# A decode step on one core: the last group's transposes ahead of the third group's normalization, its copies on two engines

## The chip, the core and the metric

The kernel runs on one core of a Trainium2 chip. A core has five engines that run side by side: TensorE (PE in the profile, with its weight loads as PEld), VectorE (DVE), ScalarE (ACT), GpSimd (POOL) and SyncE (SP), which here only issues transfers. Each has its own instruction queue, executed in order, and the queues meet at semaphores. Sixteen DMA engines bring data from the HBM memory to SBUF. TensorE writes its results to PSUM. The metric is the time of one execution in device microseconds; lower is better.

## What is computed

One token x of 576 values goes through a layer norm, and the result through two branches that are added to x. Cut to what matters:

```python
xn = _layernorm(x)
# A: attention over the last W = 4096 cached positions, 32 query heads on 16 key/value heads
q = (xn @ wq)                                  # 32 heads of 128
scores = einsum(q, k) * Dh ** -0.5
p = softmax(scores)
o = einsum(p, v)
a = o.reshape(B, Sq, Hq * Dh) @ wo
# B: gated unit, F = 4608
z = gelu(xn @ w_in); z1, z2 = z[..., :Fh], layernorm(z[..., Fh:])
b = (z1 * (w_sp * z2 + b_sp)) @ w_out
out = x + a + b
```

Everything is bf16 in memory. The keys and values of the window are 16 MB each, the weights some 17 MB more; each byte is used once.

## The kernel before

The 16 key/value heads are worked off in four groups (g = 0 to 3) of four heads. SyncE issues all large transfers in one order: wq, K of groups 0 and 1, w_in, then K and V in turn, and at the end the output weights: w_out (16 of its 18 tiles of 128 rows) and wo (32 tiles, in five transfers of 14, 9, 6, 2 and 1). Four large SBUF slots take turns, so a transfer waits until the last reader of its slot is done. The last two tiles of w_out come by two indirect transfers that GpSimd issues (`load_ext`, into `ext`).

The order of the work is written out by hand (`manual_schedule`): each engine's queue is the order of the Python calls. For each group the steps are:

- `keys` and `scores`: VectorE transposes K in blocks (L313), TensorE multiplies with the queries into S (L320).
- `sm_a`: VectorE takes the maximum over S and spreads it (L341 to L344), ScalarE writes the exponentials to `pz` and their sums to `lx` (L347).
- `sm_b`: VectorE transposes `pz` to `pt` in two instructions (L358), then ScalarE puts 32x128 pieces of `pt` in their places in `PT` with 16 copies, each from one block of 32 partitions to one block of 32 partitions (L361).
- `sums`, `recip`: TensorE adds `lx` over the partitions (L367), VectorE takes the reciprocal (L374, L375).
- `pv`: TensorE multiplies `PT` with V into the one PSUM tile `ops` (L384).
- `norm`: VectorE multiplies `ops` with the reciprocal and a mask (L394, into `om`) and adds up the columns (L398, into `on`). This frees `ops` for the next group.
- `y_mms`, `y_copy`: TensorE moves `on` to its place in a column (L405), VectorE writes it to Y (L412).

`recip`, `norm`, `y_mms` and `y_copy` together are `tail`. The small PSUM tiles (`lps`, `hx_ps`, `yps`) share one buffer (`ps_m`), so each waits until the one allocated before it has been read.

The other branch ends in `hv`, of which two columns are moved to other partitions for `ext` (`hx`). The output row is gathered in two PSUM tiles `acc` by matmuls with one column of `hv` or Y as weights (L530): `out_hv(0)`, `out_hv(1)` and `out_hv(2)` take the 16 tiles of w_out (12 + 12 + 8 matmuls), the last loop takes the 32 tiles of wo with Y, and the `ext` tiles after the 14th. Two casts (L549, L550) and one transfer bring the row out.

Of the kernel before, what the change touches and what calls it, by code (L numbers as in the profile page):

```python
# [23 lines left out]
GK = 4  # L24
NG = HKV // GK
# [20 lines left out]
def kernel(  # L46
# [14 lines left out]
    nc = tc.nc  # L61
# [243 lines left out]
    st = {}  # L305
# [45 lines left out]
    def sm_b(g):  # L351
        pt = single.tile([P, TC, 32], FP32, name=f"pt{g}", tag="pt")
        src = pz[:].rearrange("p t r x e -> p (t r x e)").bitcast(FP32)
        dst = pt[:].rearrange("p t x -> p (t x)")
        PT = work.tile([P, TC, GK, 2, 2], BF16, name=f"PT{g}", tag="PT")
        PT4 = PT[:].rearrange("p t x h e -> p (t x h e)").bitcast(FP32).rearrange("p (t x h) -> p t x h", x=GK, h=2)
        for n in range(2):
            nc.vector.transpose(dst[:, 1024 * n:1024 * (n + 1)], src[:, 1024 * n:1024 * (n + 1)])  # L358
        for x in range(GK):
            for a in range(4):  # L360
                nc.scalar.copy(PT4[32 * a:32 * a + 32, :, x, :], pt[32 * x:32 * x + 32, :, 2 * a:2 * a + 2])  # L361
        st[g]["PT"] = PT

    def sums(g):

        lps = ps_m.tile([P, 32], FP32, name=f"lps{g}", tag="m")
        nc.tensor.matmul(lps[:, 0:1], lhsT=lsum[:].rearrange("p v y e -> p (v y e)"), rhs=lx[:, g:g + 1],  # L367
                         start=True, stop=True)
        st[g]["lps"] = lps

    def recip(g):

        rs = work.tile([P, 1], FP32, name=f"rs{g}", tag="rs")
        nc.vector.tensor_scalar_max(rs[:], st[g]["lps"][:, 0:1], 0.5)  # L374
        nc.vector.reciprocal(rs[:], rs[:])  # L375
        st[g]["rs"] = rs

    def pv(g):

        d = st[g]  # L380
        for tb in range(8):
            for q in range(4):
                t0 = 32 * q + 4 * tb
                nc.tensor.matmul(  # L384
                    ops[32 * q:32 * q + 32, :],
                    lhsT=d["PT"][:, t0 // 2:t0 // 2 + 2].rearrange("p t x h e -> p (t x h e)"),
                    rhs=V[g][:, t0:t0 + 4, :],
                    start=(tb == 0), stop=(tb == 7), tile_position=(0, 32 * q),
                )

    def norm(g):
        d = st[g]
        om = work.tile([P, 4, DH], FP32, name=f"om{g}", tag="om")
        nc.vector.scalar_tensor_tensor(out=om[:].rearrange("p c d -> p (c d)"), in0=ops[:],  # L394
                                       scalar=d["rs"][:, 0:1], in1=dmask[:].rearrange("p c d -> p (c d)"),
                                       op0=ALU.mult, op1=ALU.mult)
        on = work.tile([P, DH], FP32, name=f"on{g}", tag="on")
        nc.vector.reduce_sum(on[:], om[:].rearrange("p c d -> p d c"), axis=AXX)  # L398
        d["on"] = on

    def y_mms(g):
        d = st[g]
        yps = ps_m.tile([P, 32], FP32, name=f"yps{g}", tag="m")
        for dq in range(4):
            nc.tensor.matmul(  # L405
                yps[32 * g:32 * g + 32, :], lhsT=sel[:, dq, :], rhs=d["on"][:, 32 * dq:32 * dq + 32],
                start=(dq == 0), stop=(dq == 3), tile_position=(0, 32 * g),
            )
        d["yps"] = yps

    def y_copy(g):
        nc.vector.tensor_copy(Y[32 * g:32 * g + 32, :], st[g]["yps"][32 * g:32 * g + 32, :])  # L412
# [59 lines left out]
    def tail(g):  # L472
        recip(g)
        norm(g)
        y_mms(g)
        y_copy(g)

    for g in range(2):
        for c in range(2):
# [4 lines left out]
            if g == 1 and c == 0:  # L484
                sm_a(0)
    zps = z_mms()
    sm_b(0)
    sm_a(1)
    keys(2, 0)
    scores(2, 0)  # L490
    sm_b(1)
    zg = z_exp(zps)
    keys(2, 1)
# [9 lines left out]
    pv(0)  # L503
    sm_a(2)
    tail(0)
    keys(3, 0)
    scores(3, 0)
    sm_b(2)
    sums(1)
    pv(1)  # L510
    keys(3, 1)
    scores(3, 1)
    tail(1)
    sm_a(3)
    hv = z_norm(G, sz)
    load_ext()
    sums(2)
    pv(2)
    tail(2)
    sm_b(3)  # L520
    hx_ps = ps_m.tile([P, 32], FP32, name="hx_ps", tag="m")
    nc.tensor.matmul(hx_ps[:, 0:NX], lhsT=move[:], rhs=hv[:, NM:NF], start=True, stop=True)
    hx = more.tile([P, NX], BF16, name="hx")
    nc.vector.tensor_copy(hx[:], hx_ps[:, 0:NX])  # L524
    sums(3)
    pv(3)

    def out_mms(lhs, col, wv, last):
        for n in range(2):
            nc.tensor.matmul(acc[n], lhsT=lhs[:, col:col + 1], rhs=wv[:, CUT[n]:CUT[n + 1]],  # L530
                             start=False, stop=last, tile_position=(0, 32 * n))

    def out_hv(c):
        for t, wv in wout_sb[6 * c:6 * c + 6]:
            out_mms(hv, t, wv, False)

    out_hv(0)
    out_hv(1)
    tail(3)
    out_hv(2)  # L540
    for t, wv in wo_sb:
        out_mms(Y, t, wv, t == 31)
# [39 lines left out]
```

## Time and profile before

| | us |
|---|---|
| time, median of 3 runs | 127.38 (126.96 to 127.93) |
| profiled execution, its own time | 126.47 |
| its span | 124.5 |
| VectorE busy | 80.9 (65%) |
| TensorE busy | 69.1 (55%) |
| ScalarE busy | 43.2 (35%) |
| GpSimd busy | 12.7 (10%) |
| HBM read | 51.25 MB, 412 GB/s over the span |

The span runs from the first to the last instruction of the program in one profiled execution; the execution's own time is longer by what lies around it. Times within the trace count from the span's start. In the page's list of groups a line gives the code line, engine and operation, what is written from what with partitions x elements, the count, the busy time and mean duration, and after the bar the idle time of the engine before these instructions with what ended it. In a timeline a line gives start, duration, engine, line, operation and count, and in brackets the idle time before it. The chain that ended last is followed backwards from the last instruction, at each step to what released it.

### The profile page before, as it was taken

The numbers are of one execution on the slowest core, as the hardware profiler recorded it, in microseconds if no ns is written. First come the engines' busy times: TensorE is split into PE (matmuls) and PEld (weight loads), VectorE is DVE, ScalarE is ACT, GpSimd is POOL, SyncE is SP. The second block draws the span as 40 slices with busy tenths as digits, with TensorE's granted clock in tenths as the row PEclk, the third lists the DMA queues.
The fourth block names the chain that finished last, engine by engine and source line by source line (L and its number), as shares of the span: only waits on it lengthen the run. The fifth ranks groups of instructions, "written<-read, shape, count | busy, mean of one in ns | idle before, by whom it ended". The sixth has DMA issues, their size and how long they took to land.

```text
span 124.5 us, 1494 instructions
## 1 busy us (share of the span) xinstructions
PE 69.1 (55%) x545; PEld 21.6 (17%) x545; DVE 80.9 (65%) x158; ACT 43.2 (35%) x101; POOL 12.7 (10%) x45
## 2 busy tenths in 40 slices
PE   0012851308885739999390694119995621069971
PEld 0001201301100001221000021100412311025750
DVE  6745525899599977608999628899965677104101
ACT  2100011000000783999059104913920692930001
POOL 2961730000000000000000000000000350000000
PEclk9999998555996877999959589755699995558998
DMA  4999899998989899998989999898999999999980
GB/s 116 516 424 442 366 495 390 455 474 358 500 373 451 370 511 390 453 474 369 505 358 479 400 442 463 382 495 369 484 390 447 421 421 399 435 434 403 429 316 0
DMA packets 2771, 51.04 MB, mean 410 GB/s; under 512 B 396, under 2 KB 525, under 8 KB 845
## 3 DMA queue, kind: packets, MB, share of 16 engines
q1 hardware_dynamic: 2592, 50.66, 95.2%
q0 software_dynamic: 160, 0.30, 0.6%
q8 instruction: 4, 0.07, 0.2%
q14 instruction: 3, 0.02, 0.0%
q10 hardware_dynamic: 12, 0.00, 0.0%
HBM read 51.25 MB, written 0.00 MB: 412 GB/s over the span
## 4 chain that ended last, share of the span: by engine, by line
DMA 60%; DVE 31%; PE 5%; SPq 1%; issue 1%; ACT 0%; DVEq 0%
DMA k<-in_A_k_cache_dram 37%; DMA end<-in_A_wo_dram 23%; DVE kT L313 22%; DVE pt L358 4%; PE S L320 3%; DVE om L394 1%; PE acc L530 1%; SPq L93 1%; DVE mx L341 1%; DVE on L398 1%; DVE q_rep L429 1%; PE yps L405 0%; ACT res L550 0%; DVE rs L375 0%; DVE mt L330 0%
## 5 line engine op out<-in xcount | busy, mean ns | idle before, releaser
L320 PE MATMUL S<-kT,Qb 128*8 128x512 bf16 x128 | 32.4, 1146 | 20.6 <-DVE kT L313 20.6
L313 DVE STREAM_TRANSPOSE kT<-k 128x1024 f32<-128x1024 f32 x32 | 36.8, 1207 | 6.3 <-DMA k<-in_A_k_cache_dram 6.3
L347 ACT ACTIVATE pz<-S,nm 32x1024 bf16<-32x1024 f32 x16 | 19.1, 1192 | 35.2 <-DVE nm L344 21.2
L361 ACT COPY PT<-pt 32x128 f32<-32x128 f32 x64 | 19.9, 310 | 14.5 <-DVE pt L358 13.8
L384 PE MATMUL ops<-v,PT 128*32 128x512 bf16 x128 | 9.8, 460 | 4.2 <-ACT PT L361 4.2
L320 PEld LDWEIGHTS <-Qb 128*8 128x8 bf16 x128 | 3.5, 96 | 43.1 <-issue 34.5
L358 DVE STREAM_TRANSPOSE pt<-pz 128x1024 f32<-128x1024 f32 x8 | 9.4, 1211 | 1.0 <-ACT pz L347 1.0
L462 POOL TENSOR_TENSOR mz<-mz,mhalf 128x1 f32<-128x1 f32 x1 | 0.6, 566 | 81.3 <-DVE mz L461 81.3
L394 DVE SCALAR_TENSOR_TENSOR om<-ops,rs,dmask 128x512 f32<-128x512 f32 x4 | 3.0, 750 | 7.7 <-PE ops L384 7.4
L341 DVE TENSOR_REDUCE mx<-S 128x1 f32<-128x1024 f32 x4 | 4.9, 1214 | 4.2 <-PE S L320 4.1
L421 PE MATMUL zps<-win,XZ 128*32 128x288 bf16 x56 | 7.4, 693 | 0.0
L245 ACT CAST q_rep<-qps 128x512 bf16<-128x512 f32 x2 | 1.2, 586 | 15.0 <-DVE q_rep L247 15.0
L196 PE MATMUL ps_x<-ones_b,xtw 1*128 1x1 bf16 x9 | 0.4, 162 | 8.7 <-DVE xtw L194 8.7
L530 PE MATMUL acc<-end,Y 128*1 128x264 bf16 (+1 forms) x64 | 4.8, 285 | 0.7 <-DMA end<-in_A_wo_dram 0.7
L384 PEld LDWEIGHTS <-PT 128*32 128x32 bf16 x128 | 3.5, 111 | 8.4 <-ACT PT L361 4.3
L550 ACT CAST res<-acc 1x312 bf16<-1x312 f32 x1 | 0.4, 410 | 12.0 <-PE acc L530 12.0
L367 PE MATMUL lps<-lx,lsum 128*128 128x1 f32 x8 | 1.9, 304 | 4.8 <-DVE hx L524 2.7
L405 PE MATMUL yps<-on,sel 128*32 128x32 f32 x32 | 1.7, 198 | 4.6 <-DVE on L398 4.6
L398 DVE TENSOR_REDUCE on<-om 128x128 f32<-128x512 f32 x4 | 4.2, 1041 | 0.1
L549 DVE CAST res<-acc 1x264 bf16<-1x264 f32 x1 | 0.4, 421 | 5.9 <-PE acc L530 5.9
L530 PEld LDWEIGHTS <-Y 128*1 128x1 bf16 x64 | 3.4, 83 | 1.9 <-issue 1.4
L247 DVE CAST q_rep<-qps 128x512 bf16<-128x512 f32 x2 | 1.4, 692 | 3.5 <-PE qps L236 2.8
(113 smaller groups left out, 65.6 us busy)
## 6 DMA issues: line engine op xcount, KB each, us to landing
k<-in_A_k_cache_dram SPq DMA_DIRECT2D x4, 4096.0 KB
v<-in_A_v_cache_dram SPq DMA_DIRECT2D x4, 4096.0 KB, 26.2
win<-in_B_w_in_dram SPq DMA_DIRECT2D x1, 4032.0 KB, 27.0
wq<-in_A_wq_dram SPq DMA_DIRECT2D x1, 3584.0 KB, 12.8
end<-in_B_w_out_dram SPq DMA_DIRECT2D x1, 2304.0 KB, 20.2
end<-in_A_wo_dram SPq DMA_DIRECT2D x1, 2016.0 KB
end<-in_A_wo_dram SPq DMA_DIRECT2D x1, 1296.0 KB
rest<-in_B_w_in_dram SPq DMA_DIRECT2D x1, 1152.0 KB
```

Of the source, the lines that this page charges most:

```text
L313: nc.vector.transpose(dst[:, 1024 * n:1024 * (n + 1)], src[:, 1024 * n:1024 * (n + 1)])
L320: nc.tensor.matmul(S[g % 2][32 * x:32 * x + 8, c, :], lhsT=Qb[:, GK * g + x, be].rearrange("p a h -> p (a h)"), rhs=kv[:, be // 2, be % 2, x],
L341: nc.vector.tensor_reduce(out=mx[:, 0:1], in_=s[:], op=ALU.max, axis=mybir.AxisListType.XY)
L347: nc.scalar.activation(pz[lo:hi, :, :, x, :], s[lo:hi].rearrange("p a (t r e) -> p (a t) r e", r=8, e=2), ACT.Exp, bias=nm[lo:hi, 0:1], sc ...
L358: nc.vector.transpose(dst[:, 1024 * n:1024 * (n + 1)], src[:, 1024 * n:1024 * (n + 1)])
L361: nc.scalar.copy(PT4[32 * a:32 * a + 32, :, x, :], pt[32 * x:32 * x + 32, :, 2 * a:2 * a + 2])
L367: nc.tensor.matmul(lps[:, 0:1], lhsT=lsum[:].rearrange("p v y e -> p (v y e)"), rhs=lx[:, g:g + 1], start=True, stop=True)
L384: nc.tensor.matmul(ops[32 * q:32 * q + 32, :], lhsT=d["PT"][:, t0 // 2:t0 // 2 + 2].rearrange("p t x h e -> p (t x h e)"), rhs=V[g][:, t0: ...
L394: nc.vector.scalar_tensor_tensor(out=om[:].rearrange("p c d -> p (c d)"), in0=ops[:], scalar=d["rs"][:, 0:1], in1=dmask[:].rearrange("p c ...
L398: nc.vector.reduce_sum(on[:], om[:].rearrange("p c d -> p d c"), axis=AXX)
L421: nc.tensor.matmul(zps[n][32 * q:32 * q + 32], lhsT=XZ[:, s, :], rhs=wt[:, q, ZT * n:ZT * (n + 1), :], start=(s == 0), stop=(s == NS - 1), ...
L530: nc.tensor.matmul(acc[n], lhsT=lhs[:, col:col + 1], rhs=wv[:, CUT[n]:CUT[n + 1]], start=False, stop=last, tile_position=(0, 32 * n))
```

## The change

In `sm_b` of the last group, the 16 copies are no longer issued at once on ScalarE. They are kept in a list, and a new function `sm_c` issues them in turn on VectorE and ScalarE, eight each. `norm` is split: the multiplication stays in `norm`, the addition over columns becomes `fold`. For group 2 the calls are drawn apart: its reciprocal stays, then come the transposes of group 3 and `hx`, then `norm(2)`, then group 3's `sums`, copies and reciprocal, then `fold(2)`. `y_mms(2)` and `y_copy(2)` stand behind `pv(3)`. The other groups call the same steps in the same order as before.

```diff
-        for x in range(GK):
-            for a in range(4):
-                nc.scalar.copy(PT4[32 * a:32 * a + 32, :, x, :], pt[32 * x:32 * x + 32, :, 2 * a:2 * a + 2])
         st[g]["PT"] = PT
+        st[g]["moves"] = [(PT4[32 * a:32 * a + 32, :, x, :], pt[32 * x:32 * x + 32, :, 2 * a:2 * a + 2])
+                          for x in range(GK) for a in range(4)]
+        if g < NG - 1:
+            for o, i in st[g]["moves"]:
+                nc.scalar.copy(o, i)
+
+    def sm_c(g):
+        for n, (o, i) in enumerate(st[g]["moves"]):
+            if n % 2:
+                nc.scalar.copy(o, i)
+            else:
+                nc.vector.tensor_copy(o, i)
...
+        d["om"] = om
+
+    def fold(g):
+        d = st[g]
+        om = d["om"]
         on = work.tile([P, DH], FP32, name=f"on{g}", tag="on")
         nc.vector.reduce_sum(on[:], om[:].rearrange("p c d -> p d c"), axis=AXX)
         d["on"] = on
...
     def tail(g):
         recip(g)
         norm(g)
+        fold(g)
         y_mms(g)
         y_copy(g)
...
     sums(2)
     pv(2)
-    tail(2)
+    recip(2)
     sm_b(3)
     hx_ps = ps_m.tile([P, 32], FP32, name="hx_ps", tag="m")
     nc.tensor.matmul(hx_ps[:, 0:NX], lhsT=move[:], rhs=hv[:, NM:NF], start=True, stop=True)
     hx = more.tile([P, NX], BF16, name="hx")
     nc.vector.tensor_copy(hx[:], hx_ps[:, 0:NX])
+    norm(2)
     sums(3)
+    sm_c(3)
+    recip(3)
+    fold(2)
     pv(3)
+    y_mms(2)
+    y_copy(2)
...
     out_hv(0)
     out_hv(1)
-    tail(3)
+    norm(3)
+    fold(3)
+    y_mms(3)
+    y_copy(3)
     out_hv(2)
```

## The prediction

> **What bounds the kernel now.** I read the page's header and slices first, then the chain that ended last.
>
> ```profile
> span 124.5 us, 1494 instructions
> DMA  4999899998989899998989999898999999999980
> ...
> DMA packets 2771, 51.04 MB, mean 410 GB/s; under 512 B 396, under 2 KB 525, under 8 KB 845
> ...
> 91.99 28.55 DMA end<-in_A_wo_dram
> ...
> 120.58 1.41 PE acc L530 x18
> ...
> 122.01 0.41 ACT res L550
> ```
>
> The DMA engines are at 80% or more in every slice but the first and the last two: no stage is without traffic. The chain's last long piece is the transfer of the output weights (28.55 us from issue to landing); behind it stand 18 matmuls, two casts into res and the store. The attention of group 3, which the change touches, is not on this chain. How close it comes to it, TensorE's timeline tells.
>
> ```profile
> 97.81 1.91 PE L384 MATMUL ops<-v,PT 128*32 128x512 bf16 x32
> ...
> 101.71 0.44 PE L405 MATMUL yps<-on,sel 128*32 128x32 f32 x8 [1.99 <-DVE on L398]
> ...
> 105.26 0.56 PE L367 MATMUL lps<-lx,lsum 128*128 128x1 f32 x2 [2.67 <-DVE hx L524]
> 110.03 3.47 PE L384 MATMUL ops<-v,PT 128*32 128x512 bf16 x32 [4.22 <-ACT PT L361]
> 113.34 1.76 PE L530 MATMUL acc<-end,hv 128*1 128x264 bf16 x24
> ...
> 115.70 0.58 PE L530 MATMUL acc<-end,hv 128*1 128x264 bf16 x6
> 116.16 1.75 PE L530 MATMUL acc<-end,Y 128*1 128x264 bf16 x26
> ...
> 118.52 1.39 PE L530 MATMUL acc<-end,Y 128*1 128x264 bf16 x18
> 120.58 1.38 PE L530 MATMUL acc<-end,Y 128*1 128x264 bf16 x18 [0.68 <-DMA end<-in_A_wo_dram]
> ```
>
> From 116.16 on TensorE multiplies Y by the output weights: 14 tiles, the 8 matmuls on ext, 9 tiles, then at 120.58 the last 6+2+1. The one idle time in this stretch is 0.68 us, ended by a DMA. So group 3's tail comes 0.68 us before it would set the end. That is its whole cover, and getting earlier than that is worth nothing as long as the transfers land when they do. The windows around the end show when that is.
>
> ```profile
> 120.00:120.50 0.50, 0.00 (x0) 0.00 (x0) 0.00 (x0) 0.00 (x0) 0.00 (x0) 1.00 0.88 323
> 120.50:121.00 0.50, 0.42 (x8) 0.39 (x9) 0.00 (x0) 0.00 (x0) 0.00 (x0) 1.00 0.67 240
> 121.00:121.50 0.50, 0.50 (x12) 0.42 (x9) 0.00 (x0) 0.00 (x0) 0.00 (x0) 1.00 0.18 62
> 121.50:124.50 3.00, 0.47 (x7) 0.08 (x1) 0.42 (x1) 0.41 (x1) 0.00 (x0) 0.83 0.00 0
> ```
>
> The page's transfers of the output weights, in KB, and us from issue to landing where it is known:
>
> ```profile
> end<-in_B_w_out_dram SPq DMA_DIRECT2D x1, 2304.0 KB, 20.2
> end<-in_A_wo_dram SPq DMA_DIRECT2D x1, 2016.0 KB
> end<-in_A_wo_dram SPq DMA_DIRECT2D x1, 1296.0 KB
> ...
> end<-in_A_wo_dram SPq DMA_DIRECT2D x1, 864.0 KB
> end<-in_A_wo_dram SPq DMA_DIRECT2D x1, 288.0 KB
> end<-in_A_wo_dram SPq DMA_DIRECT2D x1, 144.0 KB, 28.6
> ```
>
> In the windows the last two columns are DMA share and GB/s. Data still move at 121.0 and have stopped by 121.5; the bytes after 120.5 are (240+62) x 0.5 = 151 KB, about the size of the last issue (the 144 KB of one tile). So that tile lands between 121.0 and 121.5 and its two matmuls, the last of all, can end no earlier than some 0.3 us behind it; they end at 121.99. A tail that were infinitely early could save 0.7 us at the very most, and about 0.1 if, as the thin 62 GB/s suggests, the last packet comes near 121.3 and a matmul starts 0.3 to 0.4 us behind it.
>
> **The change part by part.** Nothing moves ahead of the reciprocal of group 2, and SP's and POOL's queues keep their contents, order and waits: each transfer waits for K, V or weight tiles whose last readers stand before the edit, and the indirect loads of ext are issued before it. So the stream of 51 MB is untouched: cost 0, since no edited instruction releases a buffer that a transfer waits for.
>
> ```profile
> 102.19 0.19 DVE L412 CAST Y<-yps 32x32 bf16<-32x32 f32 x1 [0.53 <-PE yps L405]
> 102.55 2.37 DVE L358 STREAM_TRANSPOSE pt<-pz 128x1024 f32<-128x1024 f32 x2 [0.17 <-ACT pz L347]
> 104.95 0.16 DVE L524 CAST hx<-hx_ps 128x2 bf16<-128x2 f32 x1
> 105.85 0.16 DVE L374 TENSOR_SCALAR rs<-lps 128x1 f32<-128x1 f32 x1 [0.74 <-PE lps L367]
> 106.05 0.16 DVE L375 RECIPROCAL rs<-rs 128x1 f32<-128x1 f32 x1
> 113.56 0.75 DVE L394 SCALAR_TENSOR_TENSOR om<-ops,rs,dmask 128x512 f32<-128x512 f32 x1 [7.36 <-PE ops L384]
> 114.35 1.03 DVE L398 TENSOR_REDUCE on<-om 128x128 f32<-128x512 f32 x1
> 115.91 0.20 DVE L412 CAST Y<-yps 32x32 bf16<-32x32 f32 x1 [0.53 <-PE yps L405]
> ```
>
> *Transposes ahead of norm.* Their releaser now is ScalarE's exponential (pz, 0.17 us of idle), not norm(2). Put ahead of it, VectorE waits for the same pz and starts them at 102.55 again: gain 0. They end at 102.55 + 2.37 = 104.92, and hx at 105.11. Now norm(2)'s 0.75 us stands behind them, up to 105.90: what was hidden under the exponentials delays VectorE's share of the copies.
>
> *Sixteen copies on two engines.*
>
> ```profile
> 104.95 5.03 ACT L361 COPY PT<-pt 32x128 f32<-32x128 f32 x16 [2.44 <-DVE pt L358]
> ...
> L430 DVE COPY z<-q_rep 128x36 f32<-128x36 f32 x1 | 0.2, 198 | 0.0
> L247 DVE CAST q_rep<-qps 128x512 bf16<-128x512 f32 x2 | 1.4, 692 | 3.5 <-PE qps L236 2.8 <-ACT q_rep L245 0.7
> ```
>
> ScalarE's 16 take 5.03 us, 0.314 each; its eight end at 104.95 + 2.52 = 107.47. A 32x128 f32 copy on VectorE isn't in the trace. Below stands its 36-element copy (0.198 us), above its 512-element cast (0.692 us); a line between them gives 0.198 + 92/476 x 0.494 = 0.29. I take 0.30, so eight end at 105.90 + 2.4 = 108.30 (107.5 to 111.4 by the ends). PT is complete at 108.30, where it was 109.98: 1.7 us earlier. VectorE is the later of the two.
>
> [...]
>
> *The tail behind it.* pv(3) also needs ops, which norm(2) frees at 105.90: in time; and V of group 3, behind which 2304 + 2016 + 1296 + 864 + 288 + 144 KB (7.08 MB) follow, by an estimate at 410 GB/s lands 17.3 us ahead of 121.3, near 104. It runs from 108.35 for 3.47 us to 111.82. Recip(3) (0.36) and fold(2) (1.03) follow the copies to 109.7, under pv(3), at no cost; without that cover they would cost their 1.4 us. But y_mms(2) and its cast now stand between pv(3) and norm(3): on TensorE 0.44 us, then the cast with its wait, 0.25, for which norm(3) queues on VectorE: 112.51. Before, this was done at 102.4, so these 0.69 us are added to group 3's tail. Then norm 0.78, fold 1.06, y_mms 0.50, cast 0.25: Y complete at 115.10, against 116.11 now. The 24 matmuls on hv (1.76 us) fit in between, from 112.26 to 114.0 (their weights, the 2304 KB, land 20.2 us behind their issue, which stands right ahead of the piece that the chain shows issued by 91.99), and the remaining 8 end by about 115.4. The first 14 output tiles can be there by then: behind them come 1296 + 864 + 288 + 144 KB, 2.65 MB, at 410 GB/s 6.5 us, so by this estimate they land near 114.8.
>
> *The sum.* Group 3's tail gains 1.7 - 0.7 = 1.0 us. The rest of TensorE's run, 2.36 us (116.16 to 118.52) and 1.39, then ends near 119.2 if all has landed, and TensorE waits for the same transfer, 1.4 us or less where it waited 0.68. The last 18 matmuls start at 120.58 again. Change of the span: 0 (down to -0.1). The profiled execution took 126.47 us with its span of 124.5, about 2 us around it; the median of the runs shown is 127.38, 0.9 above it. A change of 0 gives **127.3 to 127.4**; I write 127.3.
>
> **The rivals.**
>
> *VectorE's copies cost as much as the large cast* (the slower side). With a copy of c us, Y is complete at 112.70 + 8c. The cover is used up at 116.11 + 0.68 = 116.79, so c = 0.51 is where it decides. At 0.69 Y comes at 118.22, the end 1.4 us later: span 125.9, 128.8 us. For it: partitions change within the copy and the access is strided, none of which a row of VectorE shows. Against: ScalarE does the very same copy in 0.31, and the cast has four times the elements and reads PSUM. Chance 0.04.
>
> *TensorE, waiting more, loses its clock* (slower as well).
>
> ```profile
> 100.00:105.00 5.00, 0.60 (x9) 0.42 (x9) 4.23 (x6) 2.52 (x5) 1.19 (x2) 0.80 0.91 389
> 105.00:110.00 5.00, 0.56 (x2) 0.50 (x2) 0.43 (x3) 4.80 (x16) 0.00 (x0) 0.50 0.99 421
> 110.00:115.00 5.00, 4.96 (x56) 2.48 (x56) 1.40 (x2) 0.00 (x0) 0.00 (x0) 0.68 1.01 430
> 115.00:120.00 5.00, 4.56 (x71) 3.46 (x71) 0.58 (x2) 0.00 (x0) 0.00 (x0) 1.00 0.98 412
> ```
>
> Where TensorE is idle (0.56 of 5 us) the granted clock is 0.50, and the 32 matmuls of pv then took 3.47 us where at 1.00 they took 1.91: a factor of 1.8. If the last 18 matmuls met the low clock, 1.38 us would become 2.5: +1.1, 128.5 us; with the whole stretch from 115.4 (2.36 + 1.39 + 1.38) it would be 9.3 us, an end at 124.7: +2.7, 130.1. Against it: the new waits are 0.7 us more in all, and the stretch before 120 stays busy most of the time. Chance 0.06, split between the two prices. [...]
>
> *Group 3's tail is what ends last in an ordinary execution.* The runs are 0.9 us longer than the profiled one, and 0.68 us decides which of the two is last. Were the tail late in them, up to its whole 1.0 us would come out, 126.4 us. For it: nothing but the small margin; a longer run with an unbroken stream is rather one whose transfers are slower, which widens the cover. Chance 0.08; over 1% (1.27 us) it reaches only with copies as cheap as 0.2 us (another 0.8).
>
> *The change does nothing it says*: that holds for the transposes, as worked out, and is part of the forecast.
>
> **How the numbers follow.** Forecast 0.82 (no change); slow copies 0.04, low clock 0.06, late tail 0.08. One per cent is about what a measurement of this kernel can tell from no change: the three runs lie between 126.96 and 127.93. By that spread (0.5 us each side) the forecast covers 126.8 to 127.9; the range reaches down to the late tail's 126.4 and up to the cheaper clock price, 128.5. Faster by over 1%: 0.04 (part of the late tail, and scatter). Slower by over 1%: 0.09 (slow copies, most of the clock case). Within: 0.87.
>
> **What the next profile would show.** Right: pt's transposes start near 102.5 with ScalarE as releaser; eight copies of about 0.30 us on VectorE; pv(3) starts near 108.4; the last Y cast ends near 115.1; the idle time ahead of the last 18 matmuls, or the sum of such DMA waits behind the tail, grows from 0.68 to some 1.4 us; the chain still ends with the transfer of the output weights near 120.5, the span near 124.5. Wrong: matmuls on end<-Y that wait for VectorE's cast instead of a DMA; a granted clock under 1.00 between 115 and 122; an end of the transfers well off 121.3, which would mean that the stream does answer to what the engines do.

## The result and the profile after

The changed kernel takes **126.61 us** (median of 9 runs, 126.49 to 126.83) against 127.38 us before (9 runs, 126.89 to 127.93): a ratio of 0.994, 95% interval 0.9916 to 0.9965. It is faster by 0.6%, 0.8 us. What strikes more than the median is the spread: 0.34 us where it was 1.04 us.

And yet the two profiled executions are alike, 126.47 us with a span of 124.5 before, 126.61 with 124.6 after. The page after, its header and the chain that ended last:

```profile
span 124.6 us, 1493 instructions
...
DMA 60%; DVE 31%; PE 5%; SPq 1%; issue 1%; ACT 0%; DVEq 0%
...
91.37 29.32 DMA end<-in_A_wo_dram
...
120.73 1.40 PE acc L551 x18
```

The end still hangs on the output weights. TensorE's timeline after the change, from the third group's pv on:

```profile
97.99 3.41 PE L393 MATMUL ops<-v,PT 128*32 128x512 bf16 x32
...
107.56 3.61 PE L393 MATMUL ops<-v,PT 128*32 128x512 bf16 x32 [1.86 <-ACT PT L369]
...
111.34 1.64 PE L551 MATMUL acc<-end,hv 128*1 128x264 bf16 x22
113.64 0.34 PE L419 MATMUL yps<-on,sel 128*32 128x32 f32 x5 [0.66 <-DVE on L412]
...
115.55 1.75 PE L551 MATMUL acc<-end,Y 128*1 128x264 bf16 x26 [1.07 <-DMA end<-in_A_wo_dram]
...
118.65 1.36 PE L551 MATMUL acc<-end,Y 128*1 128x264 bf16 x18 [0.55 <-DMA end<-in_A_wo_dram]
120.73 1.37 PE L551 MATMUL acc<-end,Y 128*1 128x264 bf16 x18 [0.73 <-DMA end<-in_A_wo_dram]
```

Each of the three blocks on Y now waits for its transfer: 1.07 + 0.55 + 0.73 us where there was one wait of 0.68. And in the first line is what the profile before did not have: pv(2) (pv of group 2), the same 32 matmuls that took 1.91 us there, took 3.41 us here. VectorE, in the same execution:

```profile
102.58 2.37 DVE L358 STREAM_TRANSPOSE pt<-pz 128x1024 f32<-128x1024 f32 x2 [2.78 <-ACT pz L347]
104.87 0.12 DVE L539 CAST hx<-hx_ps 128x2 bf16<-128x2 f32 x1
104.92 0.73 DVE L403 SCALAR_TENSOR_TENSOR om<-ops,rs,dmask 128x512 f32<-128x512 f32 x1
105.57 1.83 DVE L371 COPY PT<-pt 32x128 f32<-32x128 f32 x8
...
111.56 0.19 DVE L426 CAST Y<-yps 32x32 bf16<-32x32 f32 x1 [2.81 <-PE yps L419]
...
114.11 0.20 DVE L426 CAST Y<-yps 32x32 bf16<-32x32 f32 x1 [0.53 <-PE yps L419]
122.12 0.42 DVE L573 CAST res<-acc 1x264 bf16<-1x264 f32 x1 [7.81 <-PE acc L551]
```

The transposes start at 102.58 although pv(2) ran to 101.40: they waited for pz alone. Behind pv(2) the old order has norm(2), y_mms(2) and a cast, 2.5 us in the profile before, ahead of them. Y is complete at 114.31, 1.8 us earlier than in the profile before.

### The profile page after: what moved, and what is told of

Read it like the earlier page. It is cut to its first block, busy times and chain, and to the rows that moved or that the text cites. A ratio compares the mean times of both kernels' runs of the same rounds, so it can differ in the third digit from the quotient of the medians.

```text
span 124.6 us, 1493 instructions
## 1 busy us (share of the span) xinstructions
PE 70.3 (56%) x545; PEld 21.9 (18%) x545; DVE 82.3 (66%) x166; ACT 40.8 (33%) x93; POOL 12.7 (10%) x45
## 4 chain that ended last, share of the span: by engine, by line
DMA 60%; DVE 31%; PE 5%; SPq 1%; issue 1%; ACT 0%; DVEq 0%
DMA k<-in_A_k_cache_dram 37%; DMA end<-in_A_wo_dram 24%; DVE kT L313 22%; DVE pt L358 4%; PE S L320 3%; PE acc L551 1%; SPq L93 1%; DVE mx L341 1%; DVE on L412 1%; DVE om L403 1%; DVE q_rep L443 1%; PE yps L419 0%; ACT res L574 0%; DVE rs L384 0%; DVE mt L330 0%
## 5 line engine op out<-in xcount | busy, mean ns | idle before, releaser
L364 ACT COPY PT<-pt 32x128 f32<-32x128 f32 x48 | 15.0, 313 | 12.0 <-DVE pt L358 11.5
L393 PE MATMUL ops<-v,PT 128*32 128x512 bf16 x128 | 10.8, 499 | 1.9 <-ACT PT L369 1.9
L426 DVE CAST Y<-yps 32x32 bf16<-32x32 f32 x4 | 0.7, 187 | 6.0 <-PE yps L419 6.0
L435 PEld LDWEIGHTS <-XZ 128*32 128x32 bf16 x72 | 2.3, 118 | 7.9 <-issue 7.9
L264 DVE TENSOR_SCALAR Qb<-qps,mask 128x32 bf16<-128x32 f32 x16 | 2.7, 352 | 1.3 <-PE qps L253 1.3
```

What stands on the lines that cost most here:

```text
L264: nc.vector.tensor_scalar_mul(qbv[:, a, h, k2], qpv[:, h, k2], mask4[:, a:a + 1])
L364: nc.scalar.copy(o, i)
L393: nc.tensor.matmul(ops[32 * q:32 * q + 32, :], lhsT=d["PT"][:, t0 // 2:t0 // 2 + 2].rearrange("p t x h e -> p (t x h e)"), rhs=V[g][:, t0: ...
L435: nc.tensor.matmul(zps[n][32 * q:32 * q + 32], lhsT=XZ[:, s, :], rhs=wt[:, q, ZT * n:ZT * (n + 1), :], start=(s == 0), stop=(s == NS - 1), ...
```

## The experiments

**The kernel before, profiled again.** No edit.

> The kernel before, unchanged, profiled once more. Two theories for the 0.8 us that the change gained. Late tail: the windows of TensorE's granted clock fall differently in each execution, so that pv(3) and the matmuls behind it often run at half clock for longer than in the profile of before; its cover of 0.68 us is then gone, and the end follows Y. Stream: the transfers themselves last longer before than after, and the tail has no part in it. Late tail expects 126.5 to 128 us with a spread of 0.5 us or more between executions, and, in any execution over 127 us, the last transfers landing near 121.3 us all the same, with the 18 last matmuls starting later than 120.6 and no DMA wait ahead of them. Stream expects the last transfers to land near 122.

Measured: 127.17 us (126.62 to 128.29), ratio to before 1.0019 (0.9982 to 1.0056). The profiled execution took 127.17 us, which is this run's median, where the first profile's took 126.47. TensorE, then VectorE:

```profile
98.03 3.39 PE L384 MATMUL ops<-v,PT 128*32 128x512 bf16 x32
103.33 0.44 PE L405 MATMUL yps<-on,sel 128*32 128x32 f32 x8 [1.92 <-DVE on L398]
...
111.52 3.60 PE L384 MATMUL ops<-v,PT 128*32 128x512 bf16 x32 [4.22 <-ACT PT L361]
...
117.78 1.75 PE L530 MATMUL acc<-end,Y 128*1 128x264 bf16 x26
...
120.14 2.57 PE L530 MATMUL acc<-end,Y 128*1 128x264 bf16 x33
```
```profile
101.47 0.75 DVE L394 SCALAR_TENSOR_TENSOR om<-ops,rs,dmask 128x512 f32<-128x512 f32 x1 [1.51 <-PE ops L384]
...
103.81 0.19 DVE L412 CAST Y<-yps 32x32 bf16<-32x32 f32 x1 [0.53 <-PE yps L405]
104.03 2.37 DVE L358 STREAM_TRANSPOSE pt<-pz 128x1024 f32<-128x1024 f32 x2
...
117.53 0.20 DVE L412 CAST Y<-yps 32x32 bf16<-32x32 f32 x1 [0.53 <-PE yps L405]
122.65 0.42 DVE L549 CAST res<-acc 1x264 bf16<-1x264 f32 x1 [4.93 <-PE acc L530]
```

pv(2) took 3.39 us, so norm(2) waited 1.51 us for it, y_mms(2) and its cast followed, and VectorE, which works in order, came to the transposes at 104.03 instead of 102.55. The exponentials had been ready since 102.74. From there everything is 1.5 to 1.6 us late: Y at 117.73, then TensorE without a single DMA wait, and the cast of the result at 122.65, where it began at 121.98 in the first profile. The expectation had looked for the lateness in pv(3); that took 3.60 us here against 3.47, and it is pv(2) that differs. In the first profile norm(2)'s row had no wait in front of it, since pv(2) had ended at 99.72:

```profile
99.85 0.75 DVE L394 SCALAR_TENSOR_TENSOR om<-ops,rs,dmask 128x512 f32<-128x512 f32 x1
```

The end of this chain shows group 3's tail in it and no transfer:

```profile
111.52 3.63 PE ops L384 x32
115.17 0.76 DVE om L394
115.96 1.05 DVE on L398
117.05 0.34 PE yps L405 x5
117.49 5.24 PE acc L530 x65
122.75 0.41 ACT res L550
```

The stream of transfers ends where it did in the first profile, as its windows show:

```profile
120.50:121.00 0.50, 0.50 (x13) 0.31 (x10) 0.00 (x0) 0.00 (x0) 0.00 (x0) 1.00 0.66 244
121.00:121.50 0.50, 0.50 (x12) 0.31 (x10) 0.00 (x0) 0.00 (x0) 0.00 (x0) 1.00 0.23 81
121.50:122.00 0.50, 0.50 (x12) 0.33 (x8) 0.00 (x0) 0.00 (x0) 0.00 (x0) 1.00 0.00 0
```

The transfers stop before 121.5, as in the first profile. That speaks against the stream and for the late tail. No execution over 127.17 us of the kernel before was profiled; what makes the longest ones, up to 128.47, is not seen in a trace.

**Group 3's tail made early.** The copies left out, pv(3) with group 2's PT:

```diff
-        for x in range(GK):
+        for x in range(GK if g < NG - 1 else 0):
...
-        st[g]["PT"] = PT
+        st[g]["PT"] = PT if g < NG - 1 else st[2]["PT"]
```

> Before, with group 3's 16 copies left out; its pv multiplies with group 2's PT instead, so that the work behind it is the same and starts some 4.5 us earlier (the attention of group 3 is not computed). The transfers are unchanged. Late tail expects the floor of the stream: 126.5 to 126.6 us, all executions within 0.4 us, as after the change. Stream expects no change from before: 127.4 us with before's spread.

Measured: 126.56 us (126.48 to 126.80), ratio 0.9937 (0.9912 to 0.9961). Y is complete at 113.45, and TensorE waits 1.87, 0.54 and 0.72 us for the three blocks of weights. This is the floor that the stream sets. The changed kernel stands 0.05 us above it, less than the spread of either.

**The copies dealt out, the order left.**

```diff
-                nc.scalar.copy(PT4[32 * a:32 * a + 32, :, x, :], pt[32 * x:32 * x + 32, :, 2 * a:2 * a + 2])
+                o, i = PT4[32 * a:32 * a + 32, :, x, :], pt[32 * x:32 * x + 32, :, 2 * a:2 * a + 2]
+                if g == NG - 1 and a % 2 == 0:
+                    nc.vector.tensor_copy(o, i)
+                else:
+                    nc.scalar.copy(o, i)
```

> Before, with only the copies of group 3 dealt to VectorE and ScalarE in turn; the order of everything else is before's, so norm(2) and y_mms(2) stay ahead of the transposes. Late tail expects PT complete at 107.5 us (ScalarE's eight, 104.95 + 2.52), Y complete near 113.6, 2.5 us earlier than before, and 126.5 to 126.6 us: all of the change's gain without its reordering. Stream expects 127.4 us.

Measured: 126.66 us (126.50 to 126.89), ratio 0.9935 (0.991 to 0.996). All of the gain, as expected, but not by the expected times: in its profile pv(2) took 3.61 us and the transposes began at 104.71, so that Y came at 116.00, not 113.6. The shorter copies make up for the late transposes; they don't prevent them.

**The order changed, the copies left on ScalarE.**

```diff
-            if n % 2:
-                nc.scalar.copy(o, i)
-            else:
-                nc.vector.tensor_copy(o, i)
+            nc.scalar.copy(o, i)
```

> The changed kernel with all 16 copies on ScalarE: the reordering alone. Late tail expects PT complete at 110.0 us as before, and Y 0.7 us later than before, since y_mms(2) and its cast now stand between pv(3) and norm(3): 128.0 us, slower than before by 0.5%. Stream expects 126.6 us if the order made the difference, 127.4 us if the copies did.

Measured: 126.67 us (126.44 to 127.34), ratio 0.9937 (0.9904 to 0.9969). The expectation of 128.0 fell. It had added 0.7 us to the first profile's 116.11, but an ordinary execution of the kernel before had Y at 117.73. VectorE's rows in this run:

```profile
102.86 2.37 DVE L358 STREAM_TRANSPOSE pt<-pz 128x1024 f32<-128x1024 f32 x2 [2.77 <-ACT pz L347]
...
113.79 0.19 DVE L423 CAST Y<-yps 32x32 bf16<-32x32 f32 x1 [6.50 <-PE yps L416]
...
116.36 0.20 DVE L423 CAST Y<-yps 32x32 bf16<-32x32 f32 x1 [0.53 <-PE yps L416]
122.23 0.42 DVE L570 CAST res<-acc 1x264 bf16<-1x264 f32 x1 [5.68 <-PE acc L548]
```

pv(2) took 2.57 us here and the transposes did not feel it. Y at 116.56 is later than in the first profile, and still early enough. So each half of the change, alone, takes the tail off the end in most executions, by the medians.

**The clock of pv(2) and of pv(3).** Matmuls on constants, into a scores buffer that is no longer read, in stretches where TensorE is idle; the first kernel has five ahead of sums(2), the second sixteen ahead of sums(3):

```diff
+    for n in range(5):
+        nc.tensor.matmul(S[0][:, n % 2, :], lhsT=ident[:], rhs=Qb[:].rearrange("p m b a h -> p (m b a h)"), start=True, stop=True)
     sums(2)
```

> Before, with five matmuls of 128x512 on constants into the idle scores buffer of group 2, put ahead of sums(2), in TensorE's idle 2.1 us there. The second profile of before showed pv(2) at half clock (3.39 us, not 1.91), and with it norm(2), y_mms(2) and the transposes 1.5 us later. Late tail through pv(2)'s clock expects: where the added work keeps the clock up, pv(2) takes 1.9 us, the transposes start near 102.6 and the time falls to 126.5 to 126.9; the slowest executions (127.9 to 128.4) become rare. If pv(2)'s clock is not what makes the tail late: 127.4 us with before's spread.

> Before, with sixteen matmuls of 128x512 on constants ahead of sums(3), in TensorE's idle 7 us between hx and pv(3). Late tail expects pv(3) at full clock, 1.9 to 2.3 us where it took 3.5, so Y 1.3 us earlier, which is about what the tail is late by in the slower executions: 126.6 to 126.9 us. If only pv(2)'s clock counted, or the tail were not the cause: 127.4 us.

Measured: 126.60 us (126.52 to 127.06), ratio 0.9953 (0.9931 to 0.9975), and 126.64 us (126.55 to 127.32), ratio 0.9953 (0.9923 to 0.9983), beside a before of 127.25 (126.60 to 128.47) on that chip. The kernel before, with useless work added and nothing taken away, gains about what the change gains. The first kernel's profile:

```profile
95.82 1.24 PE L518 MATMUL S<-Qb,ident 128*128 128x512 bf16 x4
97.98 0.38 PE L367 MATMUL lps<-lx,lsum 128*128 128x1 f32 x2 [0.92 <-DVE mz L458]
98.29 1.91 PE L384 MATMUL ops<-v,PT 128*32 128x512 bf16 x32
...
121.11 1.45 PE L532 MATMUL acc<-end,Y 128*1 128x264 bf16 x18 [0.28 <-DMA end<-in_A_wo_dram]
```

With work in front of it pv(2) takes 1.91 us. This profiled execution is the longest of its ten, 127.06 us. Its transposes began at 103.36, not near the 102.6 expected, and Y came at 117.05; yet TensorE still waited for the last weights, until 121.11, so that even here a transfer and not the tail set the end. The second kernel's profile, at 127.32 us also its longest, shows pv(2) at 3.52 us and pv(3) at 3.48 us, not the 1.9 to 2.3 expected: TensorE was idle for 2.03 us ahead of pv(3), and the granted clock, 0.70 on the mean from 110 to 115, fell to 0.50 at 112.0, 0.2 us after its start. None of its eight executions at 126.55 to 126.73 was profiled, so what pv(3) took in those stays open.

**A later tail in the changed kernel.** Group 3's transposes, two more of them in the first kernel (shown), three more in the second:

```diff
-        for n in range(2):
+        for n in range(2 if g < NG - 1 else 4):
+            n %= 2
             nc.vector.transpose(dst[:, 1024 * n:1024 * (n + 1)], src[:, 1024 * n:1024 * (n + 1)])
```

> The changed kernel with group 3's two transposes done a second time ahead of the copies: 2 x 1.19 = 2.37 us added to its tail, nothing else. Late tail: the profile after the change leaves TensorE 3.75 us of matmuls from 114.5, so Y's last cast may come 2.4 us later before the wait at 120.73 is used up: 126.6 to 126.8 us. Had the change gained by something other than the lateness of Y: the same. A cover as small as the forecast's 1.7 us (0.68 + 1.0): 127.3 us.

> The changed kernel with one more transpose than the run with two: 3 x 1.19 = 3.56 us added. Late tail: 1.1 us beyond the cover of 2.45 us, 127.7 us. Stream (the tail has no part in the time): 126.6 us.

Measured: 126.75 us (126.44 to 127.25), ratio 0.9974 (0.9953 to 0.9994), and 127.40 us (126.63 to 127.96), ratio 1.0009 (0.9971 to 1.0048). The expectations were 126.6 to 126.8 and 127.7. The first 2.37 us cost 0.14 us over the changed kernel's 126.61 (measured apart from these, beside a before of 127.38 instead of 127.25), the next 1.19 us another 0.65: a cover that ends near 2.4 us, and a cost behind it. In the second one's profile (127.68 us), Y is complete at 118.25:

```profile
118.05 0.20 DVE L427 CAST Y<-yps 32x32 bf16<-32x32 f32 x1 [0.53 <-PE yps L420]
123.17 0.42 DVE L574 CAST res<-acc 1x264 bf16<-1x264 f32 x1 [4.93 <-PE acc L552]
```

From the end of Y's cast to the cast of the result it is 123.17 - 118.25 = 4.92 us. In the kernel before profiled again it is 122.65 - 117.73 = 4.92 us, and in the run with sixteen matmuls 122.79 - 117.86 = 4.93 us: wherever no transfer is waited for, the end is Y plus 4.92. In eight other profiles the cast of the result begins at 121.95 to 122.25, whatever Y does between 113.45 and 116.56. So the end is the later of two things, the stream's 121.95 to 122.25, and Y + 4.92; they cross at a Y between 117.0 and 117.3. The profile with the five matmuls shows that the stream itself varies: Y at 117.05 would put the cast at 121.97, and it began at 122.58, behind the DMA wait of 0.28 us. There the transfers moved at 79 GB/s on the mean from 120.0 to 124.5, where the first profile has 70.

**A smaller last piece, beside the changed kernel again.**

```diff
-(6, 0, NF), (2, 0, NF + 6)
+(3, 0, NF), (3, 0, NF + 3), (2, 0, NF + 6)
```

> The changed kernel with the transfer of 6 tiles of wo drawn apart into two of 3 tiles. After the change only the transfers set the end: the last 18 matmuls wait for the 6 tiles until 120.7 and then need 1.4 us, while the very last tile lands near 121.3. With the first 3 tiles there earlier, 6 of the 18 matmuls go ahead, and the last two can end some 0.3 us behind the last landing's wait, near 121.9 to 122.0: 0.1 to 0.2 us less than the changed kernel, 126.4 to 126.5 us. If the end hangs on the last landing alone: no change, 126.6 us.

> The changed kernel, unchanged, on this chip beside the run with smaller pieces and in five rounds. Late tail expects 126.5 to 126.7 us, all executions within 0.4 us, whatever the granted clock of pv(2); beside it before with its 126.6 to 128.4.

Measured: with smaller pieces 126.92 us (126.81 to 127.09), the changed kernel 126.69 us (126.55 to 126.89), before 127.12 us (126.69 to 128.40); ratios to before 0.9971 (0.9944 to 0.9998) and 0.995 (0.9921 to 0.998). The edit lost 0.23 us instead of gaining 0.1 to 0.2.

```profile
118.65 1.75 PE L551 MATMUL acc<-end,Y 128*1 128x264 bf16 x24 [0.54 <-DMA end<-in_A_wo_dram]
120.86 1.36 PE L551 MATMUL acc<-end,Y 128*1 128x264 bf16 x12 [0.46 <-DMA end<-in_A_wo_dram]
```

Six more matmuls do go ahead, but the other 12 wait until 120.86 and don't end earlier for it: the cast of the result began at 122.24, against 122.25 in the changed kernel beside it. The transfers of this run move at 157 GB/s from 121.0 to 121.5 and at 0 from there to 122.0, with six matmuls in that last half microsecond, so the end hangs on the last landing, the case for which no change was expected. The loss lies behind the cast: from its start to the end of the span it is 125.0 - 122.24 = 2.76 us here, and 2.47 to 2.55 us in the eleven other profiles. Why the divided transfer lengthens that stretch stays open. The changed kernel repeated its time, and no version tried here beats it clearly.

## Why the prediction was right and where it was not

The time lies in the range, and the change is within 1%, as forecast. But the forecast was no change, since the stream sets the end, and the interval excludes no change: what happened is the rival that had 0.08, group 3's tail as what ends last in an ordinary execution, at the 0.8 us between the medians instead of the 1.0 it was given. The number fits because the range reaches down to that rival's 126.4; the mechanism of the forecast did not hold for the median execution.

- *The stream untouched, the end no earlier than it allows.* Right. The transfers stop before 121.5 in the windows of the first profiles of both kernels, and the floor with the tail far ahead is 126.56 us.
- *The cover of 0.68 us.* Read correctly from its row, and true for that execution alone. With a pv(2) of 3.39 us, as in the second profile of the kernel before, the cover was gone: Y at 117.73 against the 117.0 to 117.3 at which it starts to cost.
- *Transposes ahead of norm: gain 0.* This is the step that failed. It took the 0.17 us of idle as what ties the transposes to pz, and so saw nothing else to wait for. In that profile norm(2) had begun at 99.85, right behind a pv(2) of 1.91 us. With pv(2) at 3.4 us, VectorE's queue gets to the transposes only at 104.03. The move takes them out from behind pv(2). With the old order they began at 102.55 and 103.36 behind a pv(2) of 1.91 us, and at 104.03 to 104.71 in the four profiles where it took 3.30 to 3.61 us. With the new order they began at 102.58 to 103.04 in all six profiles, with pv(2) anywhere from 1.91 to 3.61 us.
- *Copies.* VectorE's 32x128 copy took 0.218 us on the mean, against 0.30 assumed; eight took 1.83 us. PT was complete at 107.50, set by ScalarE, not by VectorE at 108.30: VectorE was done at 107.40. The rival of a dear copy had its point of decision at 0.51 us and falls. The forecast counted eight whole durations one behind the other, an estimate. Measured, 1.83 us for eight is 0.229 us each, more than the 0.201 to 0.225 us that single copies took, so these eight did not overlap. The first of them started at 105.57, 0.08 us ahead of om's end at 105.65.
- *The tail behind it.* The 0.69 us of y_mms(2) and its cast are there: norm(3) begins at 111.78, 0.61 us behind pv(3)'s end at 111.17, after the cast at 111.56 that waits for TensorE. Y came at 114.31, forecast 115.10; the difference is the copies'. Mostly for the same reason TensorE's waits for transfers behind the tail came to 2.35 us, not to some 1.4. The first of them, 1.07 us, also shows that the first 14 output tiles were there only near 115.5; the estimate from 410 GB/s had them near 114.8.
- *A lower clock through waiting.* Wrong in its place. The granted clock after the change was 1.00 from 115 to the end, with waits of 1.07, 0.55 and 0.73 us in that stretch; the clock that mattered was pv(2)'s, in the kernel before (3.39 us in its second profile, with a granted clock of 0.83 on the mean from 95 to 100; 1.91 us in its first, with 1.00). The 0.50 that the prediction read from 105 to 110, around a wait of 4.22 us, does not tell what a wait costs: in that profile the clock had fallen before it, at 103.0, 1.3 us behind the end of a wait of 1.99 us (to 101.71). After the change it fell at 97.7, when the wait just ended was 2.11 us. The same wait of 2.11 us ahead of pv(2) left the clock at 1.00 in the profile before. So the clock fell behind two of these three waits of some 2 us and not behind the third; whether 1.4 us can cost it is not shown.
- *The argument against the right rival* was "a longer run with an unbroken stream is rather one whose transfers are slower". Nothing in the profile bore this out, and the second profile of before refutes it for that execution. A hint was there: the profiled execution, at 126.47 us, was faster than every run of the kernel before that was shown (126.96 to 127.93), so that its slack was nearer the best case than the usual one.

When the granted clock falls and rises was not controlled in any run. That a pv(2) of 3.30 to 3.61 us delays group 3's transposes in the old order is shown by the profiles, and that before's tail ends last in ordinary executions by the second profile, by the floor and by the later tails. That pv(2) is the main reason is borne out by taking the dependence away (the order alone) and by a pv(2) with the clock up (five matmuls: a granted clock of 1.00 from 95 to 100, pv(2) in 1.91 us). It isn't the only lever: the sixteen matmuls behind pv(2) gave the same median. The runs themselves tie the time to the clock: of the kernel before's 93 executions in these experiments, on three chips, the 19 with a mean granted clock of 0.837 or 0.838 took 127.23 to 128.47 us, the 14 at 0.809 or 0.810 took 126.87 to 127.75. So a higher mean is not a shorter time. That it depends on which matmuls meet the slow stretches fits this, and is not shown for the longest executions. How the executions between 126.6 and 128.5 us divide among the clocks of pv(2), of pv(3) and of the matmuls on hv was not measured.

## What to carry to other kernels

A slack of 0.7 us read from one profile is one execution's. Compare the profiled execution's own time with the spread of the runs first: if it is faster than all of them, a chain that it shows as just early may be late in the others. On an engine that works in order, put a step that is ready by another engine's signal ahead of one that waits for matmuls of varying speed (here 1.91 to 3.61 us for the same 32); room against variation can be worth more than one profile shows. And where a stream of transfers sets the floor, stop once the spread is as narrow as the floor's.

## What the runs showed that was not expected

The same 32 matmuls of pv(2) took 1.91, 2.57, 3.39, 3.41 and 3.61 us, among others, in different executions. The profile page's line of granted clocks (40 equal slices of the span, in tenths of full speed) goes with this: in the profile of the kernel before, and in its second profile,

```profile
PEclk9999998555996877999959589755699995558998
```
```profile
PEclk9999996555699595999777569955999777555999
```

the stretches at half clock lie in other places against the same program. Five matmuls without use, put into an idle gap ahead of pv(2), took 0.65 us off the kernel's median on one chip; work that adds nothing made this kernel faster.
